# Sliding-window attention feeding a gated MLP: batch 2 transposed by TensorE, batch 3's x^T by DMA, and PSUM homes moved at the end of tile 0

## The chip, the cores and the metric

The kernel runs on one core of a Trainium2 chip. The metric is the device time of one execution in microseconds; of several executions the median is given. The engines of the core work side by side, each on its own queue in program order: TensorE (PE, matrix products and transposes, results to PSUM), VectorE (DVE), ScalarE (ACT), GpSimd (POOL, here casts and DMA issues) and SyncE (SP, here DMA issues).

## What is computed

Attention over a causal window of 64 positions, for 8 batches, 8 heads, 576 positions and head size 64; its output, as 4608 rows of 512, goes through two weight matrices with a gate between them.

```
scores = scale * np.matmul(q, k.transpose(0, 1, 3, 2))
rel = pos[:, None] - pos[None, :]
mask = (rel >= 0) & (rel < window)
...
attn_out = np.matmul(attn, v)
x = np.ascontiguousarray(attn_out.transpose(0, 2, 1, 3)).reshape(B * S, H * D)
h = x @ w_in
g = h * np.clip(h + 3.0, 0.0, 6.0) / 6.0
out = g @ w_out
```

Here w_in is 512 x 2048 and w_out is 2048 x 512. All inputs and the output are float32; the kernel multiplies in bf16.

## The kernel before

The MLP works on 9 tiles of 512 rows (T = 0 to 8), the attention on 8 batches of 576 rows, each as 4 pairs of heads (g = 0 to 3). The order of all work is written by hand: the kernel turns automatic scheduling off, so each engine does its instructions in the order of the code, and only the waits between engines are put in automatically.

**A tile.** Stage 1 (`s1`) makes 16 blocks of 128 hidden units: four matmuls over xT and w_in into a PSUM bank, then the gate: ACT writes relu(h/6 + 1/2), and DVE takes its minimum with 1, times h, into gT. Stage 2 (`s2`) makes 4 output blocks of 128 rows, each in 4 quarters of four matmuls over gT and w_out; ACT copies a finished block to SBUF (`osb`), and SP writes it out (those of tile 0 are held back for POOL's queue).

**A batch.** q, k and v are loaded (SP, for the first two batches partly POOL), cast to bf16 by POOL into `qn_all`, `kn_all` and V, and q and k are transposed into QT and KT, either by PE (`TT` for a pair: four transposes each of q and k, copied from PSUM by DVE and ACT; `RR` for the 64 rows of each that the 512 of the main part leave) or by a DMA transpose on SP. `SS` makes a pair's scores in st0 and st1, takes exp on ACT and masks on DVE. `N_` multiplies with V, both heads of a pair, and DVE normalizes into `opg`. x^T, the input of stage 1, is made from opg by `X_` (five transposes on PE, a copy by ACT) or by `xt_dma` (a DMA transpose on SP).

**What is laid between what.** `stage_(T, ...)` runs stage 1 and stage 2 of a tile, and after block or quarter i it runs the attention pieces that `pieces` lists for i. Tile T carries the attention of batch T + 1. Tile 0 is written out by hand: its stage 2 carries batch 1 and the rest of batch 0. In tiles 1 and 2 of the kernel before, the first four blocks of stage 1 are computed over part of xT first, with pair 3's `X_` in between (`s1` with `first`).

**Data of batches 1 to 4.** Batch 1 comes in rows of 1 KB (`LoadsForPE`, four positions of a head in a row) and is transposed by PE. Batch 2 comes in blocks of 128 positions with rows of 256 bytes (`load_for_dma`: 5 DMAs each for q, k and v), is cast by `cast_for_dma`, and `transpose_pairs_by_dma` issues 8 DMA transposes for it on SP. The loads for batch 3 stand behind them on SP's queue. Batch 3 and those after it are transposed by two DMAs each (`transpose_by_dma`). x^T of batches 0 to 3 is made by PE, that of batches 4 to 7 by DMA.

**PSUM.** Eight banks: st0 and st1 are tiles of two banks each ([P, 2, 512] in float32 or [P, 2, 1024] in bf16), o and acc one bank each, and two h banks that are taken in turn (`h_bank`, `h_tr`). `oa` and `oa_tr` hand out o and acc in turn; `st_tr(u)` and `st_pair(u)` hand out the two halves of st0 or st1. `s1_bank` says where a block of stage 1 is computed; in tile 1 blocks 4 to 15 are in h, h, st0, st1, h, h, st0, st1, o, acc, h, h.

Of the kernel before, what the change touches and what calls it, by code (L numbers as in the profile page):

```python
# [10 lines left out]
BF16 = mybir.dt.bfloat16  # L11
# [13 lines left out]
def kernel(  # L25
# [9 lines left out]
    nc = tc.nc  # L35
    P = nc.NUM_PARTITIONS
# [3 lines left out]
    NG = H // 2  # L40
# [57 lines left out]
        return out  # L98

    class LoadsForPE:  # L100
        def __init__(self, b):
            self.b = b
            self.qst = stage.tile([P, H, R * D], F32, name="qst", tag="qst")
            self.kst = stage.tile([P, H, R * D], F32, name="kst", tag="kst")
            self.rst = stage.tile([P, H, D], F32, name="rst", tag="rst")
            self.tiles = (self.qst, self.kst, self.rst)

        def main(self, i, h0, h1):
            nc.gpsimd.dma_start(
                out=self.tiles[i][:, h0:h1, :],  # L110
                in_=(q, k)[i][self.b, h0:h1, 0:SM, :].rearrange("h (p j) d -> p h (j d)", j=R),
            )

        def rest(self):
            for i, src in enumerate((q, k)):
                nc.gpsimd.dma_start(
                    out=self.rst[i * SR : (i + 1) * SR, :, :],
                    in_=src[self.b, :, SM:S, :].rearrange("h s d -> s h d"),
                )

    def load_v_by_head(b):
        vst = stage.tile([P, KB, H, D], F32, name="vst", tag="vst")
        ins = load_blocks(vst, v, b, (KB - 1,), SR) + load_v(b, vst, 0, H)
        return vst, ins

    def load_for_dma(b):
        sts, ins = [], []
        for n, src in (("qst", q), ("kst", k), ("vst", v)):
            t = stage.tile([P, KB, H, D], F32, name=n, tag=n)
            ins += load_blocks(t, src, b, range(KB), SR if src is v else 0)  # L130
            sts.append(t)
        return tuple(sts), ins
# [108 lines left out]
    class Batch:  # L241
# [28 lines left out]
        def transpose_by_dma(self):  # L270
            for n, T in ((qn_all, self.QT), (kn_all, self.KT)):
# [1 line left out]
                    out=T[:].rearrange("d g (k s) -> d (g k) s", s=P),  # L273
                    in_=n[:].rearrange("p g k h d -> p (g k h d)"),
                )

        def transpose_pairs_by_dma(self):
            for g in range(NG):
                for n, T in ((qn_all, self.QT), (kn_all, self.KT)):
                    nc.sync.dma_start_transpose(  # L280
                        out=T[:, g, :].rearrange("d (k s) -> d k s", s=P),
                        in_=n[:, g, :, :, :].rearrange("p k h d -> p (k h d)"),
                    )

        def cast_qk(self, st, i, h0, heads, copy):
            n = (qn_all, kn_all)[i][:].rearrange("p g k h d -> p (g k h d)")[:, 0 : R * H * D]
# [126 lines left out]
    def xt_pe(bt, g, tr):  # L413
        opg = opgs.pop((bt.b, g))
        n = S if bt.b else SM
        for qb in range(KB if bt.b else KB - 1):
            nc.tensor.transpose(  # L417
                out=tr[:, qb * P : (qb + 1) * P],
                in_=opg[:, qb, :, :].rearrange("p h d -> p (h d)"),
                identity=ident[:],  # L420
            )
        return lambda: acopy(out=xT[:, g, bt.b * S : bt.b * S + n], in_=tr[:, 0:n])
# [38 lines left out]
    def rest_x(bt, u):  # L461
        tr = ps_st.tile([P, 2, 1024], BF16, name=f"st{u}")[:, 0, :]
        for g in range(NG):
            nc.tensor.transpose(
                out=tr[:, g * SR : (g + 1) * SR],
                in_=opr[0:SR, g, :, :].rearrange("p h d -> p (h d)"), identity=ident[0:SR, 0:SR],
            )
        acopy(
            out=xT[:, :, bt.b * S + SM : (bt.b + 1) * S],
            in_=tr[:, 0 : NG * SR].rearrange("d (g s) -> d g s", s=SR),  # L470
        )
# [19 lines left out]
    def h_tr():  # L491
        return ps_h.tile([P, 1024], BF16, name=h_name())
# [31 lines left out]
    def s1(T, first=()):  # L524
        t0 = T * TB
        gT = gpool.tile([P, NFC, TB], BF16, name="gT")
        gTs[T] = gT

        def mms(fc, hT, gs):
            for g in gs:  # L530
                nc.tensor.matmul(  # L531
                    hT, lhsT=win16[:, g, fc * P : (fc + 1) * P],
                    rhs=xT[:, g, t0 : t0 + TB], start=(g == 0), stop=(g == NG - 1),
                )

        def gate(out, hT, shape):
            t1 = (t1pool, t2pool)[len(shape) - 2].tile(shape, BF16, name=f"t{len(shape) - 1}")
            nc.scalar.activation(out=t1[:], in_=hT, func=RELU, bias=half[:], scale=1.0 / 6.0)  # L538
            nc.vector.scalar_tensor_tensor(  # L539
                out=out, in0=t1[:], scalar=1.0, in1=hT, op0=MIN, op1=MULT,  # L540
            )

        if first:
            sts = [ps_st.tile([P, 2, 512], F32, name=f"st{u}") for u in range(2)]
            for gs in first:
                for fc in range(4):
                    mms(fc, sts[fc // 2][:, fc % 2, :], gs)
                yield
            for u in range(2):
                for fc in (2 * u, 2 * u + 1):  # L550
                    mms(fc, sts[u][:, fc % 2, :], (NG - 1,))
                gate(gT[:, 2 * u : 2 * u + 2, :], sts[u][:], [P, 2, TB])
                yield
                yield
        for fc in range(4 if first else 0, NFC):
            hT = s1_bank(fc, T)
            mms(fc, hT, range(NG))
            gate(gT[:, fc, :], hT, [P, TB])
            yield
# [53 lines left out]
    def N_(bt, g, banks=None):  # L613
        n = [pv(bt, g, h, next(banks) if banks else h_bank()) for h in range(2)]
        n[0]()
        n[1]()

    def X_(bt, g, st=None):
        xt_pe(bt, g, h_tr() if st is None else ps_st.tile([P, 2, 1024], BF16, name=f"st{st}")[:, 0, :])()

    def TT(bt, g, banks=None):
        T_(bt, g, banks)
# [118 lines left out]
    bt.cast_v_end(vst1, pcopy)  # L741
    for g in range(NG):
        bt.cast_v(vst1, 2 * g, 2 * g + 2, pcopy)
    st2, _ = load_for_dma(2)

    def st_tr(u):
        t = ps_st.tile([P, 2, 1024], BF16, name=f"st{u}")
# [2 lines left out]
    def st_pair(u):  # L750
        t = ps_st.tile([P, 2, 512], F32, name=f"st{u}")
        return iter((t[:, 0, :], t[:, 1, :]))
# [7 lines left out]
    def go(n=1):  # L760
        run(m, n)
# [6 lines left out]
    S1_(0, 1, 1)  # L768
    go()
    S1_(1, 1, 0)  # L770
    go()
    TT(bt, 2, st_tr(1))
    go()
    TT(bt, 3, st_tr(0))
    go()
    S1_(2, 0, 1)
# [13 lines left out]
    N_(bt, 0, st_pair(0))  # L790
    go()
    N_(bt, 1, oa)
    rest_x(bt0, 1)
    go()
    X_(bt, 0)
    N_(bt, 2, st_pair(0))
    X_(bt, 1, 1)
    N_(bt, 3, oa)
    X_(bt, 2)

    def stage_(T, bt, pieces1, pieces2):
        if T < 3:
            m = s1(T, ((0, 1), (2,)))
            run(m, 1)
            X_(Batch(T), NG - 1)
            run(m, 1)
        else:
            m = s1(T)
        for i in range(NFC):
            run(m, 1)  # L810
            for f in pieces1.get(i, ()):
                f()
        m = s2(T, BY_BLOCK)
        for i in range(16):
            run(m, 1)
            for f in pieces2.get(i, ()):
                f()

    def pieces(bt):
        if bt is None:  # L820
            return {}, {}
        f = lambda fn, *a: lambda: fn(bt, *a)
        p1, p2 = {}, {}
        if bt.b == 2:
            return p1, {
                1: [f(SS, 0)], 2: [f(SS, 1)], 4: [f(N_, 0), f(SS, 2)], 6: [f(X_, 0)], 7: [f(N_, 1), f(SS, 3)],
                9: [f(X_, 1)], 10: [f(N_, 2)], 12: [f(X_, 2)], 13: [f(N_, 3)],
            }
        if bt.b == 3:
            return {13: [f(SS, 0)]}, {  # L830
                0: [f(SS, 1)], 3: [f(N_, 0), f(SS, 2)], 5: [f(X_, 0)], 6: [f(N_, 1), f(SS, 3)],
                8: [f(X_, 1)], 9: [f(N_, 2)], 11: [f(X_, 2)], 12: [f(N_, 3)], 14: [f(X_, 3)],
            }
        p1 = {10: [f(SS, 0)], 13: [f(SS, 1)]}
        p2 = {
            0: [f(SS, 2)], 1: [f(N_, 0)], 2: [f(SS, 3)], 3: [f(N_, 1), f(xt_dma, 0)],
            5: [f(xt_dma, 1)], 6: [f(N_, 2)], 8: [f(N_, 3), f(xt_dma, 2)], 10: [f(xt_dma, 3)],
        }
        return p1, p2

    bt2 = Batch(2)
    bt2.cast_for_dma(st2, (0, 1))
    for u0, osb in held:
        nc.gpsimd.dma_start(out=out[u0 : u0 + P, :], in_=osb[:])
    bt2.cast_for_dma(st2, (2,))
    bt2.transpose_pairs_by_dma()
    nxt, pend = bt2, None
    for T in range(1, NTB):
        p1, p2 = pieces(nxt)
        b = T + 2  # L850
        nxt = None
        if b < B:
            sts, _ = load_for_dma(b)
            nxt = Batch(b)
            p1.setdefault(12 if T == 1 else 6, []).append(
                lambda bt=nxt, sts=sts: bt.cast_for_dma(sts)
            )
            p2.setdefault(6 if T < 3 else 12, []).append(lambda bt=nxt: bt.transpose_by_dma())
        stage_(T, None, p1, p2)


# [28 lines left out]
```

The softmax here doesn't subtract the row's maximum and nothing guards it: scores larger than these inputs give would overflow.

## Time and profile before

| what | value |
|---|---|
| median of 7 runs | 314.17 us (312.67 to 315.31) |
| the profiled execution | 314.43 us, span 312.7 us |
| DMA moved | 52.80 MB, mean 169 GB/s |
| matmuls of stage 2 into o and acc (L568) | 64.1 us and 62.4 us busy |
| matmuls of stage 1 into h (L531) | 62.8 us busy |
| POOL's idle time before its casts of q (L258) | 71.4 us, of it 55.2 us until loads of q landed |
| DMA issues of q, k and v on SP, 256 KB each | 4.7 us, 5.6 us and 5.5 us to landing (median) |
| DMA transposes QT and KT on SP | 9 each, 4.4 us to landing (median) |
| DMA transposes of x^T on SP | 16, 2.9 us to landing (median) |

The span is the time from the first to the last instruction of the profiled execution; the run's own time lies 1.7 us above it. Busy time counts the time in which an engine has an instruction under way. A name such as L322 is a line of the kernel; "gT<-t,st" reads as output from inputs. In a timeline a row has its start, its duration and, in brackets, the idle time of its engine just before it with the instruction that ended that wait. In a table by windows, the columns are the stretch, its length, then busy time and number of instructions of PE, PE's weight loads, DVE, ACT and POOL, then the granted share of PE's clock, the DMA share and GB/s.

### The profile page before, as it was taken

The page shows a single profiled execution, that of the slowest core. Times are in us where ns is not written, and L with a number is a line of the kernel's source. Part 1 is how long each engine was busy: PE and PEld are TensorE (multiplying, and loading weights), DVE is VectorE, ACT ScalarE, POOL GpSimd, SP SyncE. Part 2 cuts the span into 40 slices and gives each one's busy share as a digit, 9 for nine tenths or more (in the row PEclk, how much of TensorE's full clock was granted, in tenths as well). Part 3 has the DMA queues.
Part 4 walks back from the last instruction along what each step waited for, and adds up shares of the span by engine and source line. Part 5 has one row for each costly group of instructions (what it writes and reads, how often), then busy time and mean ns, then how long its engine had stood idle before and what let it go on. Part 6 is the DMA issues. An engine that isn't in the chain of part 4 may idle for free.

```text
span 312.7 us, 5579 instructions
## 1 busy us (share of the span) xinstructions
PE 299.3 (96%) x2125; PEld 148.1 (47%) x2162; DVE 174.8 (56%) x334; ACT 177.4 (57%) x264; POOL 92.2 (29%) x137
## 2 busy tenths in 40 slices
PE   8899898999999999999999999999999999999995
PEld 3454345544654455445544554455445544444442
DVE  4569445485636754478447753775377527306700
ACT  3858654587627854796158715881588157317611
POOL 5876616373044243305600660075000000000000
PEclk9999999999999999999999999999999999999999
DMA  7999999998899999999999999999900630010011
GB/s 243 209 219 238 244 204 201 198 202 220 168 199 199 277 215 195 221 244 203 210 231 212 204 202 230 213 213 190 249 8 2 133 88 0 34 69 34 0 69 67
DMA packets 147579, 52.80 MB, mean 169 GB/s; under 512 B 136384, under 2 KB 142528, under 8 KB 147552
## 3 DMA queue, kind: packets, MB, share of 16 engines
q1 hardware_dynamic: 141920, 44.18, 70.4%
q0 software_dynamic: 5360, 8.00, 12.6%
q8 instruction: 17, 0.28, 0.4%
q10 hardware_dynamic: 272, 0.26, 0.2%
q14 instruction: 10, 0.08, 0.1%
HBM read 36.70 MB, written 9.44 MB: 148 GB/s over the span
## 4 chain that ended last, share of the span: by engine, by line
PE 73%; DMA 14%; SPq 4%; POOL 3%; DVE 2%; ACT 1%; issue 1%; POOLq 0%
PE o L568 17%; PE acc L568 16%; PE h L531 15%; PE o L531 5%; PE acc L531 5%; PE st L531 5%; DMA wout<-in_moe_w_out_dram 4%; PE st L354 3%; DMA kst<-in_k_dram 3%; DMA qst<-in_q_dram 3%; DMA vst<-in_v_dram 3%; SPq L94 2%; PE h L384 2%; DMA KT<-kn 1%; PE h L389 1%
## 5 line engine op out<-in xcount | busy, mean ns | idle before, releaser
L531 PEld LDWEIGHTS <-win 128*128 128x128 bf16 x576 | 55.2, 98 | 66.8 <-issue 1.6
L568 PEld LDWEIGHTS <-gT 128*128 128x128 bf16 x576 | 52.4, 98 | 57.2 <-issue 1.0
L568 PE MATMUL o<-wout,gT 128*128 128x512 bf16 x261 | 64.1, 380 | 1.4 <-DMA wout<-in_moe_w_out_dram 0.6
L531 PE MATMUL h<-xT,win 128*128 128x512 bf16 x259 | 62.8, 379 | 0.3
L568 PE MATMUL acc<-wout,gT 128*128 128x512 bf16 x261 | 62.4, 379 | 0.6
L362 ACT ACTIVATE pT<-st 128x768 bf16<-128x768 f32 x64 | 48.7, 808 | 14.2 <-PE st L354 14.1
L539 DVE SCALAR_TENSOR_TENSOR gT<-t,st 128x512 bf16<-128x512 bf16 (+1 forms) x26 | 20.7, 809 | 57.1 <-ACT t L538 57.0
L538 ACT ACTIVATE t<-h,half 128x512 bf16<-128x512 f32 x66 | 44.7, 690 | 8.4 <-PE h L531 7.9
L539 DVE SCALAR_TENSOR_TENSOR gT<-t,h 128x512 bf16<-128x512 bf16 x66 | 44.5, 685 | 7.9 <-ACT t L538 7.7
L372 DVE TENSOR_TENSOR pT<-pT,mask 128x1536 bf16<-128x1536 bf16 x28 | 28.3, 1011 | 22.6 <-ACT pT L362 22.6
L258 POOL CAST qn<-qst 128x512 bf16<-128x512 f32 x24 | 16.6, 730 | 71.4 <-DMA qst<-in_q_dram 55.2
L574 ACT COPY osb<-acc 128x512 f32<-128x512 f32 x17 | 10.0, 586 | 41.2 <-PE acc L568 41.2
L531 PE MATMUL st<-xT,win 128*128 128x512 bf16 x124 | 29.9, 379 | 0.9 <-DVE gT L539 0.3
L574 ACT COPY osb<-o 128x512 f32<-128x512 f32 x17 | 10.0, 588 | 30.4 <-PE o L568 30.4
L406 DVE TENSOR_TENSOR opg<-h,rec 128x320 bf16<-128x320 f32 x48 | 23.6, 491 | 1.7
L531 PE MATMUL o<-xT,win 128*128 128x512 bf16 x91 | 23.6, 379 | 0.4 <-DVE gT L539 0.3
L538 ACT ACTIVATE t<-st,half 128x512 bf16<-128x512 f32 (+1 forms) x26 | 20.1, 785 | 6.7 <-PE st L531 6.4
L531 PE MATMUL acc<-xT,win 128*128 128x512 bf16 x90 | 23.5, 379 | 0.1
L248 POOL CAST V<-vst 128x512 bf16<-128x512 f32 (+1 forms) x14 | 16.6, 1189 | 16.9 <-DMA vst<-in_v_dram 14.3
L384 PEld LDWEIGHTS <-pT 128*128 128x128 bf16 x256 | 17.4, 97 | 7.6 <-PE h L417 0.5
L258 POOL CAST kn<-kst 128x512 bf16<-128x512 f32 x24 | 14.6, 648 | 17.7 <-DMA kst<-in_k_dram 14.0
L354 PE MATMUL st<-QT,KT 64*128 64x192 bf16 (+2 forms) x312 | 17.5, 230 | 1.6 <-DMA KT<-kn 0.7
(107 smaller groups left out, 282.3 us busy)
## 6 DMA issues: line engine op xcount, KB each, us to landing
out_dram<-osb SPq DMA_DIRECT2D x32, 256.0 KB, 2.5
qst<-in_q_dram SPq DMA_DIRECT2D x28, 256.0 KB, 4.7
kst<-in_k_dram SPq DMA_DIRECT2D x27, 256.0 KB, 5.6
vst<-in_v_dram SPq DMA_DIRECT2D x24, 256.0 KB, 5.5
vst<-in_v_dram SPq DMA_DIRECT2D x23, 128.0 KB, 3.6
win<-in_moe_w_in_dram POOLq DMA_DIRECT2D x4, 512.0 KB, 8.0
wout<-in_moe_w_out_dram POOLq DMA_DIRECT2D x4, 512.0 KB, 13.0
qst<-in_q_dram POOLq DMA_DIRECT2D x2, 512.0 KB, 11.9
```

Source lines behind the costliest of these rows:

```text
L248: copy(out=self.V[:, 0 : KB - 1, h0:h1, 0:D], in_=vst[:, 0 : KB - 1, h0:h1, :])
L258: pcopy(out=n[:, g, 0 : KB - 1, :, :].rearrange("p k h d -> p k (h d)"), in_=s[:, 0 : KB - 1, 2 * g : 2 * g + 2, :].rearrange("p k h d -> ...
L354: nc.tensor.matmul(st[:, h, o0 : o0 + n], lhsT=bt.KT[h * D : (h + 1) * D, g, k0 : k0 + P], rhs=bt.QT[h * D : (h + 1) * D, g, q0 : q0 + n], ...
L362: nc.scalar.activation(out=pT[:, :, 2 * u : 2 * u + 2, 0:QW], in_=st[:, :, 0:w].rearrange("p h (k w) -> p h k w", k=2), func=EXP, scale=scale,
L372: nc.vector.tensor_tensor(out=pT[:, :, :, 0:QW], in0=pT[:, :, :, 0:QW], in1=mask[:].rearrange("p (h k) w -> p h k w", h=2), op=MULT,)
L384: nc.tensor.matmul(ob, lhsT=pT[:, h, qb, 0:P], rhs=V[:, qb, 2 * g + h, :], start=True, stop=(qb == 0),)
L406: nc.vector.tensor_tensor(out=opgs[bt.b, g][:, 0:nb, h, :], in0=ov[:, :, 0:D], in1=rec[:, 0:nb].unsqueeze(2).to_broadcast([P, nb, D]), op= ...
L531: nc.tensor.matmul(hT, lhsT=win16[:, g, fc * P : (fc + 1) * P], rhs=xT[:, g, t0 : t0 + TB], start=(g == 0), stop=(g == NG - 1),)
L538: nc.scalar.activation(out=t1[:], in_=hT, func=RELU, bias=half[:], scale=1.0 / 6.0)
L539: nc.vector.scalar_tensor_tensor(out=out, in0=t1[:], scalar=1.0, in1=hT, op0=MIN, op1=MULT,)
L568: nc.tensor.matmul(accs[ts], lhsT=gT[:, fc, ts * P : (ts + 1) * P], rhs=wout16[:, fc, :], start=(fc == 0), stop=(fc == NFC - 1),)
L574: acopy(out=osb[:], in_=accs[ts])
```

## The change

- Batch 2 is loaded as batch 1 is, in rows of 1 KB, but on SP's queue (`LoadsForPE` gets an engine), q and k for the first four heads first; V comes head by head. It is cast by `cast_pairs` and `cast_rest`.
- Its 8 DMA transposes go (`transpose_pairs_by_dma` is removed). PE transposes it in tile 1: pairs 0 and 1 in stage 1 after blocks 6 and 10, in o and acc; pairs 2 and 3 and the remaining rows in stage 2 after quarters 0, 3 and 1, in the h banks. Its scores and products move one or two quarters later.
- Batch 3 loses its own list of pieces and gets that of the later batches: scores after blocks 10 and 13 of tile 2's stage 1, x^T by four DMAs on SP. Its casts are placed in tile 1's stage 2 after quarter 6, its DMA transposes after quarter 8; those of batch 4 move to stage 2's quarter 12.
- At the end of tile 0: `TT` of batch 1's pair 2 stands one quarter earlier; `rest_x` of batch 0 uses st0; `X_` of pairs 0 and 1 share the tile st1; `N_` of pair 2 uses o and acc, of pair 3 the h banks; `X_` of pairs 2 and 3 move into tile 1, where the first four blocks of stage 1 are computed over xT group 0, then 1, then 2. Tile 2 is cut in the same way, with `X_` of batch 2's pairs 2 and 3.

```diff
--- before.py
+++ after.py
@@ -98,22 +98,22 @@
         return out
 
     class LoadsForPE:
-        def __init__(self, b):
-            self.b = b
+        def __init__(self, b, eng=None):
+            self.b, self.eng = b, eng or nc.gpsimd
             self.qst = stage.tile([P, H, R * D], F32, name="qst", tag="qst")
             self.kst = stage.tile([P, H, R * D], F32, name="kst", tag="kst")
             self.rst = stage.tile([P, H, D], F32, name="rst", tag="rst")
             self.tiles = (self.qst, self.kst, self.rst)
 
         def main(self, i, h0, h1):
-            nc.gpsimd.dma_start(
+            self.eng.dma_start(
                 out=self.tiles[i][:, h0:h1, :],
                 in_=(q, k)[i][self.b, h0:h1, 0:SM, :].rearrange("h (p j) d -> p h (j d)", j=R),
             )
 
         def rest(self):
             for i, src in enumerate((q, k)):
-                nc.gpsimd.dma_start(
+                self.eng.dma_start(
                     out=self.rst[i * SR : (i + 1) * SR, :, :],
                     in_=src[self.b, :, SM:S, :].rearrange("h s d -> s h d"),
                 )
@@ -274,14 +274,6 @@
                     in_=n[:].rearrange("p g k h d -> p (g k h d)"),
                 )
 
-        def transpose_pairs_by_dma(self):
-            for g in range(NG):
-                for n, T in ((qn_all, self.QT), (kn_all, self.KT)):
-                    nc.sync.dma_start_transpose(
-                        out=T[:, g, :].rearrange("d (k s) -> d k s", s=P),
-                        in_=n[:, g, :, :, :].rearrange("p k h d -> p (k h d)"),
-                    )
-
         def cast_qk(self, st, i, h0, heads, copy):
             n = (qn_all, kn_all)[i][:].rearrange("p g k h d -> p (g k h d)")[:, 0 : R * H * D]
             copy(
@@ -615,8 +607,8 @@
         n[0]()
         n[1]()
 
-    def X_(bt, g, st=None):
-        xt_pe(bt, g, h_tr() if st is None else ps_st.tile([P, 2, 1024], BF16, name=f"st{st}")[:, 0, :])()
+    def X_(bt, g, banks=None):
+        xt_pe(bt, g, next(banks) if banks else h_tr())()
 
     def TT(bt, g, banks=None):
         T_(bt, g, banks)
@@ -741,7 +733,14 @@
     bt.cast_v_end(vst1, pcopy)
     for g in range(NG):
         bt.cast_v(vst1, 2 * g, 2 * g + 2, pcopy)
-    st2, _ = load_for_dma(2)
+    ld = LoadsForPE(2, nc.sync)
+    ld.main(0, 0, 4)
+    ld.main(1, 0, 4)
+    ld.rest()
+    ld.main(0, 4, 8)
+    ld.main(1, 4, 8)
+    st2 = ld.tiles
+    vst2, _ = load_v_by_head(2)
 
     def st_tr(u):
         t = ps_st.tile([P, 2, 1024], BF16, name=f"st{u}")
@@ -768,9 +767,8 @@
     S1_(0, 1, 1)
     go()
     S1_(1, 1, 0)
-    go()
     TT(bt, 2, st_tr(1))
-    go()
+    go(2)
     TT(bt, 3, st_tr(0))
     go()
     S1_(2, 0, 1)
@@ -790,19 +788,28 @@
     N_(bt, 0, st_pair(0))
     go()
     N_(bt, 1, oa)
-    rest_x(bt0, 1)
-    go()
-    X_(bt, 0)
-    N_(bt, 2, st_pair(0))
-    X_(bt, 1, 1)
-    N_(bt, 3, oa)
-    X_(bt, 2)
+    rest_x(bt0, 0)
+    go()
+    two = st_tr(1)
+    X_(bt, 0, two)
+    X_(bt, 1, two)
+    N_(bt, 2, oa)
+    N_(bt, 3)
 
     def stage_(T, bt, pieces1, pieces2):
-        if T < 3:
-            m = s1(T, ((0, 1), (2,)))
+        if T == 1:
+            m = s1(T, ((0,), (1,), (2,)))
             run(m, 1)
-            X_(Batch(T), NG - 1)
+            X_(Batch(1), 2, oa_tr)
+            run(m, 1)
+            X_(Batch(1), 3, oa_tr)
+            run(m, 1)
+        elif T == 2:
+            m = s1(T, ((0,), (1,), (2,)))
+            run(m, 1)
+            X_(Batch(2), 2)
+            run(m, 1)
+            X_(Batch(2), 3)
             run(m, 1)
         else:
             m = s1(T)
@@ -822,14 +829,10 @@
         f = lambda fn, *a: lambda: fn(bt, *a)
         p1, p2 = {}, {}
         if bt.b == 2:
-            return p1, {
-                1: [f(SS, 0)], 2: [f(SS, 1)], 4: [f(N_, 0), f(SS, 2)], 6: [f(X_, 0)], 7: [f(N_, 1), f(SS, 3)],
-                9: [f(X_, 1)], 10: [f(N_, 2)], 12: [f(X_, 2)], 13: [f(N_, 3)],
-            }
-        if bt.b == 3:
-            return {13: [f(SS, 0)]}, {
-                0: [f(SS, 1)], 3: [f(N_, 0), f(SS, 2)], 5: [f(X_, 0)], 6: [f(N_, 1), f(SS, 3)],
-                8: [f(X_, 1)], 9: [f(N_, 2)], 11: [f(X_, 2)], 12: [f(N_, 3)], 14: [f(X_, 3)],
+            return {6: [f(TT, 0, oa_tr)], 10: [f(TT, 1, oa_tr)]}, {
+                0: [f(TT, 2)], 1: [f(RR)], 2: [f(SS, 0)], 3: [f(TT, 3)], 4: [f(SS, 1)],
+                6: [f(N_, 0), f(SS, 2)], 8: [f(X_, 0)], 9: [f(N_, 1), f(SS, 3)],
+                11: [f(X_, 1)], 12: [f(N_, 2)], 14: [f(N_, 3)],
             }
         p1 = {10: [f(SS, 0)], 13: [f(SS, 1)]}
         p2 = {
@@ -839,11 +842,14 @@
         return p1, p2
 
     bt2 = Batch(2)
-    bt2.cast_for_dma(st2, (0, 1))
+    cast_pairs(bt2, st2, 0, 4)
+    bt2.cast_rest(st2, pcopy)
+    cast_pairs(bt2, st2, 4, 4)
     for u0, osb in held:
         nc.gpsimd.dma_start(out=out[u0 : u0 + P, :], in_=osb[:])
-    bt2.cast_for_dma(st2, (2,))
-    bt2.transpose_pairs_by_dma()
+    bt2.cast_v_end(vst2, pcopy)
+    for g in range(NG):
+        bt2.cast_v(vst2, 2 * g, 2 * g + 2, pcopy)
     nxt, pend = bt2, None
     for T in range(1, NTB):
         p1, p2 = pieces(nxt)
@@ -852,10 +858,10 @@
         if b < B:
             sts, _ = load_for_dma(b)
             nxt = Batch(b)
-            p1.setdefault(12 if T == 1 else 6, []).append(
+            (p2 if T == 1 else p1).setdefault(6, []).append(
                 lambda bt=nxt, sts=sts: bt.cast_for_dma(sts)
             )
-            p2.setdefault(6 if T < 3 else 12, []).append(lambda bt=nxt: bt.transpose_by_dma())
+            p2.setdefault(8 if T == 1 else 12, []).append(lambda bt=nxt: bt.transpose_by_dma())
         stage_(T, None, p1, p2)
 
 
```

## The prediction

> **What bounds the kernel now.** I read the engine rows first, then busy time by stage, then PE's timeline, then what ACT and DVE do where PE's order changes.
>
> ```profile
> span 312.7 us, 5579 instructions
> PE 299.3 (96%) x2125; PEld 148.1 (47%) x2162; DVE 174.8 (56%) x334; ACT 177.4 (57%) x264; POOL 92.2 (29%) x137
> ...
> 38.90:58.70 19.80, 17.47 (x190) 9.84 (x191) 11.64 (x29) 9.96 (x16) 7.08 (x14) 1.00 1.14 201
> 94.80:108.00 13.20, 12.14 (x64) 5.42 (x64) 9.16 (x13) 10.61 (x16) 4.52 (x6) 1.00 1.02 235
> 158.40:190.10 31.70, 31.49 (x229) 15.58 (x232) 19.67 (x36) 18.50 (x28) 10.24 (x13) 1.00 1.11 212
> ```
>
> PE (first busy column) is the bound at the full granted clock. A later tile is busy 31.49 of 31.70 us. Where the change acts, PE idles 2.33 us in 38.9 to 58.7 and 1.06 us in 94.8 to 108.0. By the first matmuls of each stage 1, tile 1 lasts from 58.07 to 92.06 (33.99 us), tile 2 to about 126.62 (34.56), tile 3 to 158.38 (31.76). So there is little to win: a saving counts only if it takes work or a recorded wait from PE, and a new PE wait counts in full.
>
> ```profile
> 39.53 1.02 PE L568 MATMUL o<-wout,gT 128*128 128x512 bf16 x4 [0.59 <-DMA wout<-in_moe_w_out_dram]
> 40.39 0.39 PE L317 MATMUL st<-ident,qn 128*128 128x128 bf16 x4
> 40.61 0.39 PE L317 MATMUL st<-ident,kn 128*128 128x128 bf16 x4
> 40.83 1.03 PE L568 MATMUL acc<-wout,gT 128*128 128x512 bf16 x4
> ...
> 57.78 0.45 PE L417 MATMUL h<-ident,opg 128*128 128x128 bf16 x5 [0.67 <-DVE opg L406]
> ...
> 105.78 0.51 PE L354 MATMUL st<-QT,KT 64*128 64x192 bf16 x10 [0.70 <-DMA KT<-kn]
> ```
>
> Columns are start, duration, instruction, and in brackets the idle time with its releaser. Eight transposes run from 40.39 to 40.83, so one costs 55 ns of PE; a quarter block of stage 2 (four matmuls) costs 0.86 us. The three brackets are the waits that the change can reach.
>
> **PE work.** Batch 2 on PE needs 4 pairs x 2 x 4 transposes and 4 for the remaining rows: 36 x 0.055 = +1.98 us, all in tile 1. Batch 3's x^T by DMA takes 4 x 5 away: 20 x 0.055 = -1.10 us, in tile 2. The other x^T groups only change places. Net +0.88 us. A rule speaks against this trade: the Trainium skill ("TensorE: Matmul & The Clock Gate", Part 4: PE-mode transpose) gives about 275 ns for a 128x128 bf16 transpose inside a kernel. Sixteen more would be 4.4 us by that figure and 0.88 by the row. The row decides: it is start to start, in this kernel, between the same matmuls.
>
> **Waits that go.** (1) Moving the transposes of batch 1's pair 2 ahead of the quarter block that waits for w_out fills that gap: the previous scores end near 38.9, the bank st1 is free (its exp ran 37.73 to 38.54), the weights land at 39.48 either way, so the 0.44 us of transposes come free: -0.44. (2) X of pair 2 in batch 1 waited 0.67 for DVE; now four matmuls of tile 1 stand in front of it: -0.67. X of pair 3, behind four more, should still wait about 0.1 for its own normalization: +0.12. (3) Batch 3's scores waited 0.70 for KT at 105.78. Its loads were issued from 79.22 on, because SP had eight transposes of batch 2 in front. Those are gone; SP can issue batch 3's loads as soon as the tiles are cast, near 60 to 76. Its POOL casts now stand behind PE's last read of qn (about 80), two casts of 2.9 us follow, then two SP transposes of some 3 us each with landing: about 93, where scores now start near 106. -0.70. (4) Two score groups one quarter apart cost 0.20 at 76.68 (waiting on the exp); they now stand two apart: -0.20. Together -1.89, with X of pair 3 included.
>
> **New waits**, all for a PSUM bank. These rows of ACT and DVE carry them:
>
> ```profile
> 41.03 0.69 DVE L322 COPY QT<-st 128x512 bf16<-128x512 bf16 x1 [0.26 <-PE st L317]
> ...
> 41.76 0.58 ACT L322 COPY KT<-st 128x512 bf16<-128x512 bf16 x1 [1.97 <-DVE QT L322]
> ...
> 55.62 0.58 ACT L574 COPY osb<-h 128x512 f32<-128x512 f32 x1 [0.60 <-PE h L568]
> 56.10 0.65 ACT L422 COPY xT<-h 128x576 bf16<-128x576 bf16 x1
> ...
> 69.52 0.69 DVE L539 SCALAR_TENSOR_TENSOR gT<-t,st 128x512 bf16<-128x512 bf16 x1 [0.18 <-ACT t L538]
> ...
> 73.84 0.69 DVE L539 SCALAR_TENSOR_TENSOR gT<-t,h 128x512 bf16<-128x512 bf16 x1 [0.18 <-ACT t L538]
> ```
>
> (a) X of pairs 0 and 1 of batch 1 get the two halves of st1. The first two rows show such a tile: q's transposes in one half, k's in the other. DVE's copy of q waited for k's transposes (end 40.83), and ACT's copy of k waited for DVE's copy of q (41.72): the tile is handed over as a whole. Then pair 1's transposes wait until ACT has copied pair 0: transposes end 55.69, ACT is still at the output block, its copy runs 56.10 to 56.75, PE goes on at 56.80: +1.1 us. Queued behind it are N of pairs 2 and 3 and the whole of tile 1. The skill's rule ("PSUM — Partial Sum Buffer", PSUM bank collisions raise a hardware error) is to guard by bank; halves of 2 KB are two banks, so by the rule this wait would be 0 and the total +0.7 us, by the row +1.8. I take the row: it is the same kind of tile, twice in the trace. Ends 0 and 1.1.
>
> (b) In tile 1's stage 1, pair 1 of batch 2 is transposed into o and acc after block 10, and block 12 is computed in o. DVE copies q only after block 10's gate (it starts at 69.52; queued operations follow 0.60 apart): copy 70.12 to 70.81, PE at 70.87. PE would come to block 12 at 69.46 + 0.44 = 69.90: +0.97 us. Pair 0 after block 6 has no block in o or acc behind it; DVE takes its 0.60 in the 0.26 us a block has spare. Ends 0 and 1.2.
>
> (c) Pair 2 goes to the h banks after the first quarter of stage 2, while block 15's gate still reads one: 73.84 + 0.69, so PE may go on at 74.6 and stands ready at 72.92 + 0.86 + 0.22 = 74.0: +0.61. Ends 0.4 and 0.8.
>
> (d) The remaining rows are copied by DVE (0.28) and then ACT (0.37) out of one bank; with 0.2 before and 0.1 behind, that is 0.96 us against the 0.86 us quarter that covers it: +0.10. The moved rest_x, now in st0, waits for a normalization that ended at 54.43 where it stood at 54.32: under 0.1, nothing.
>
> **Behind other work.** Batch 2's loads: SP begins them at 49.69. POOL's 512 KB loads with 1 KB rows landed 1.45 us apart (35.72, 37.16), SP's 256 KB blocks 1.2 us apart. So pairs 0 and 1 of q and k land near 56, are cast (1.04 us each) by 58, the rest by 62; PE asks at about 64.2 and, for pair 2, at 74. Cover 6 us. V is cast by 70, behind the four output issues of POOL, and asked for after 81. The x^T DMAs of batch 3 stand on SP behind batch 4's loads, which start near 95 and not at 105.77, so SP is free near 113 when the first is due; in tile 3 the same four issued as late as 151.10 to 155.73 and the last landed at 158.33, just in time for 158.38. The casts of batch 4 also move earlier. No gain follows in tiles 3 to 8: their PE has 0.2 us of idle time each.
>
> **Sum.** +0.88 of work, -1.89 of waits, new waits 1.1 + 0.97 + 0.61 + 0.10 = +2.78: **+1.8 us** on the profiled execution's 314.43 (span 312.7 and 1.7 around it) is 316.2; on the median of 314.17 it is **316.0 us**.
>
> **Rivals.** *Halves tracked apart*: only (a) goes, +0.7, 314.9 us; for it, the halves are different banks; against it, the KT row. *Data late*: if the SP loads behaved like POOL's in the weight phase (11.9 us to landing, against 3.4 to 6.3 on SP), q and k of pairs 0 and 1 would be cast near 64 and those after them near 70, each a few us later than I put it; from about 7 us later on PE stops in stage 1, and 2 us of that give 318. Against it: the weights have landed by 46.7. *Faster*: the PSUM homes are free in time, because DVE takes q's copies ahead of gates that still wait for ACT and PE comes later to the shared banks: then work +0.88 and -2.01 remain, 313.0 us. It decides once the new waits are below 0.2 us together; for it, DVE is only 56% busy; against it, DVE's order is fixed by hand, gate first.
>
> **Chances.** The sum above 0.58, halves apart 0.20, faster 0.12, data late 0.10. What can be told from no change here is 0.3%, 0.94 us either side of 314.17. The first case lies mostly above 315.1 (0.53 of 0.58), halves apart mostly within the band (0.13 of 0.20, the rest above), data late above: slower 0.69, same 0.19, faster 0.12. The likeliest case alone spans 315.0 to 317.2; the range to hold eight in ten reaches down into the second case and up towards the late data: 313.9 to 317.6.
>
> **What would show it.** After: pair 1's X transposes idle about 1.1 us, released by ACT's xT copy; block 12 into o idle 1 us, released by QT; k's transposes of pair 2 idle 0.6, released by gT; no wait of L354 for KT by DMA; tile 1 near 37.6 us long, tile 2 near 32.7, tile 3 unchanged at 31.8. I am wrong if PE waits on POOL or on loads in tile 1, if the bank waits are absent, or if tile 2 keeps its length.

## The result, and the profile after

The changed kernel takes 316.08 us (median of 26 executions, 314.74 to 318.17); the kernel before, run beside it, 314.17 us (63 executions). The ratio is 1.0063, with a 95% interval of 1.0047 to 1.0079: about 2.0 us slower, between 1.5 and 2.5.

In the changed kernel the line numbers have moved: L523 is a matmul of stage 1, L560 of stage 2, L309 a transpose of q or k, L409 one of x^T, L364 the masked product. Its page begins:

```profile
span 316.4 us, 5620 instructions
PE 301.9 (95%) x2140; PEld 149.5 (47%) x2178; DVE 178.2 (56%) x339; ACT 176.6 (56%) x265; POOL 97.9 (31%) x138
```

Its busy time by stage (columns as before, PE is the first busy one; the rows are stage 2 of tile 0, tile 1 and tile 2):

```profile
37.03:59.92 22.89, 21.02 (x213) 11.23 (x216) 11.19 (x26) 12.55 (x20) 9.13 (x15) 1.00 1.08 213
59.92:96.93 37.01, 35.09 (x288) 18.83 (x291) 25.07 (x46) 22.59 (x34) 20.92 (x30) 1.00 1.11 215
96.93:129.82 32.89, 32.28 (x240) 16.20 (x242) 19.36 (x35) 18.82 (x28) 10.22 (x13) 1.00 1.00 181
```

PE is busy 2.6 us longer than before, over a span that is 3.7 us longer. Tile 2 is 1.7 us shorter, tile 1 is 3.0 us longer. These are waits in PE's timeline that the profile before does not have. The change made the last three; the first, for the weights w_in, is not its work:

```profile
20.02 3.10 PE L523 MATMUL st<-xT,win 128*128 128x512 bf16 x7 [1.83 <-DMA win<-in_moe_w_in_dram]
...
58.67 0.44 PE L409 MATMUL st<-ident,opg 128*128 128x128 bf16 x5 [0.94 <-ACT xT L414]
...
73.30 1.02 PE L523 MATMUL o<-xT,win 128*128 128x512 bf16 x4 [0.79 <-DVE QT L314]
...
78.41 0.38 PE L309 MATMUL h<-ident,kn 128*128 128x128 bf16 x4 [0.41 <-DVE gT L531]
```

At 58.67 the second x^T of the shared tile waits for ACT's copy of the first; at 73.30 block 12 waits in o for DVE's copy of q; at 78.41 pair 2's k waits for the gate of block 15. The wait for KT by DMA is gone. In this one execution w_in came late, and PE then ran at half its clock for a while; that is no part of the change (the section on the hardware comes back to it). Two more profiles of the same kernel show PE busy for 300.9 and 300.4 us, 1.6 and 1.1 us more than before. Lengths in us, from the first matmul of each stage to the next:

| stretch | before | after | after, 2nd | after, 3rd |
|---|---|---|---|---|
| start to stage 2 of tile 0 | 33.63 | 37.03 | 33.44 | 33.90 |
| stage 2 of tile 0 | 24.44 | 22.89 | 23.56 | 23.00 |
| tile 1 | 33.99 | 37.01 | 37.02 | 37.02 |
| tile 2 | 34.62 | 32.89 | 33.92 | 33.81 |
| tile 3 to the end | 186.02 | 186.55 | 186.97 | 186.66 |

Tile 1 is the same to 0.01 us in all three. Tile 2 is not, and why is the second question of the experiments.

### The profile page after: what moved, and what is told of

It reads as the page before. It is cut to its first block, busy times and chain, and to the rows that moved or that the text cites. A ratio compares the mean times of both kernels' runs of the same rounds, so it can differ in the third digit from the quotient of the medians.

```text
span 316.4 us, 5620 instructions
## 1 busy us (share of the span) xinstructions
PE 301.9 (95%) x2140; PEld 149.5 (47%) x2178; DVE 178.2 (56%) x339; ACT 176.6 (56%) x265; POOL 97.9 (31%) x138
## 4 chain that ended last, share of the span: by engine, by line
PE 85%; DMA 7%; DVE 2%; ACT 2%; SPq 2%; issue 1%; POOL 0%; POOLq 0%
PE acc L560 18%; PE o L560 18%; PE h L523 17%; PE st L523 8%; PE acc L523 6%; PE o L523 6%; PE st L346 4%; DMA qst<-in_q_dram 3%; DMA win<-in_moe_w_in_dram 2%; PE h L376 2%; PE h L381 1%; PE h L560 1%; SPq L94 1%; DMA vst<-in_v_dram 1%; DVE gT L531 1%
## 5 line engine op out<-in xcount | busy, mean ns | idle before, releaser
L523 PEld LDWEIGHTS <-win 128*128 128x128 bf16 x576 | 55.4, 98 | 68.3 <-issue 3.7
L560 PEld LDWEIGHTS <-gT 128*128 128x128 bf16 x576 | 52.5, 98 | 57.0 <-issue 0.5
L560 PE MATMUL o<-wout,gT 128*128 128x512 bf16 x261 | 64.3, 380 | 0.6 <-issue 0.2
L523 PE MATMUL h<-xT,win 128*128 128x512 bf16 x259 | 63.0, 379 | 0.3
L560 PE MATMUL acc<-wout,gT 128*128 128x512 bf16 x261 | 61.9, 379 | 0.7 <-issue 0.2
L531 DVE SCALAR_TENSOR_TENSOR gT<-t,st 128x512 bf16<-128x512 bf16 (+1 forms) x26 | 20.7, 808 | 61.9 <-ACT t L530 61.8
L364 DVE TENSOR_TENSOR pT<-pT,mask 128x1536 bf16<-128x1536 bf16 x28 | 30.3, 1083 | 20.9 <-ACT pT L354 20.8
L258 POOL CAST qn<-qst 128x512 bf16<-128x512 f32 x20 | 13.0, 689 | 71.8 <-DMA qst<-in_q_dram 46.5
L523 PE MATMUL st<-xT,win 128*128 128x512 bf16 x124 | 32.1, 393 | 2.3 <-DMA win<-in_moe_w_in_dram 1.8
L398 DVE TENSOR_TENSOR opg<-h,rec 128x320 bf16<-128x320 f32 x50 | 24.6, 491 | 1.7
L523 PE MATMUL o<-xT,win 128*128 128x512 bf16 x91 | 23.6, 379 | 1.1 <-DVE QT L314 0.8
L523 PE MATMUL acc<-xT,win 128*128 128x512 bf16 x89 | 23.5, 379 | 0.2
L248 POOL CAST V<-vst 128x512 bf16<-128x512 f32 (+1 forms) x17 | 18.1, 1067 | 14.1 <-DMA vst<-in_v_dram 10.7
L258 POOL CAST kn<-kst 128x512 bf16<-128x512 f32 x20 | 15.3, 802 | 10.7 <-DMA kst<-in_k_dram 10.7
L346 PEld LDWEIGHTS <-KT 64*128 64x128 bf16 x312 | 10.9, 94 | 15.7 <-issue 12.7
```

The costliest lines, as they stand in the source:

```text
L248: copy(out=self.V[:, 0 : KB - 1, h0:h1, 0:D], in_=vst[:, 0 : KB - 1, h0:h1, :])
L258: pcopy(out=n[:, g, 0 : KB - 1, :, :].rearrange("p k h d -> p k (h d)"), in_=s[:, 0 : KB - 1, 2 * g : 2 * g + 2, :].rearrange("p k h d -> ...
L346: nc.tensor.matmul(st[:, h, o0 : o0 + n], lhsT=bt.KT[h * D : (h + 1) * D, g, k0 : k0 + P], rhs=bt.QT[h * D : (h + 1) * D, g, q0 : q0 + n], ...
L364: nc.vector.tensor_tensor(out=pT[:, :, :, 0:QW], in0=pT[:, :, :, 0:QW], in1=mask[:].rearrange("p (h k) w -> p h k w", h=2), op=MULT,)
L398: nc.vector.tensor_tensor(out=opgs[bt.b, g][:, 0:nb, h, :], in0=ov[:, :, 0:D], in1=rec[:, 0:nb].unsqueeze(2).to_broadcast([P, nb, D]), op= ...
L523: nc.tensor.matmul(hT, lhsT=win16[:, g, fc * P : (fc + 1) * P], rhs=xT[:, g, t0 : t0 + TB], start=(g == 0), stop=(g == NG - 1),)
```

## The experiments

Eleven runs were made, in three groups (the first four, the next four, the last three), each group on one chip with the kernel before beside it. All ratios are to the kernel before. The three profiles of the kernel after stand above: the second is the first run here, the third is the ninth.

**The changed kernel again.**

> The changed kernel again, as the measure for the three others on the same chip. My theory (three new PSUM waits, then work, make up the loss): about 316.1 us, ratio 1.006 to the kernel before, with the waits of 0.9, 0.8 and 0.4 us that the changed profile shows. Rival (the loss lies in the start: the changed profile shows a wait of 1.83 us for w_in at 20.02, which the kernel before did not have): the late w_in is there again and the start up to the first quarter of tile 0's stage 2 is some 2 us longer than before.

316.4 us, ratio 1.0064 (1.0046 to 1.0082). The start was 33.44 us long, no longer than before, and the waits of 0.94, 0.79 and 0.41 us were all there. The loss isn't in the start.

**Own tiles for the two x^T.**

```diff
-    two = st_tr(1)
-    X_(bt, 0, two)
-    X_(bt, 1, two)
+    X_(bt, 0, st_tr(0))
+    X_(bt, 1, st_tr(1))
```

> X of pairs 0 and 1 of batch 1 get a tile of their own each (first half of st0, first half of st1). My theory: the wait of 0.94 us of the second X for ACT's copy of the first goes, nothing takes its place, about 315.1 us (ratio 1.003). Rival (halves are free of each other, and the wait was ACT being late with the output block): the wait stays in another form and the time stays at 316.1. Rival (the start): 316.1.

315.61 us, ratio 1.0038 (1.0019 to 1.0057). The wait of 0.94 us is gone and none stands in its place (one of 0.69 us earlier in the stage, for batch 0's KT, is 0.24 in the changed kernel's profiles and varies); tile 1 is unchanged at 37.01. In time it is 0.8 us less, though the intervals of the two kernels overlap. Same two engines, same order, only separate tiles: ACT's lateness alone was not the cause.

**Other banks for blocks 12 to 15.**

```diff
-        if fc in (12, 13):
-            return (ps_o, ps_acc)[fc - 12].tile([P, 512], F32, name=("o", "acc")[fc - 12])[:]
         if fc % 4 < 2:
             return h_bank()[:]
-        return ps_st.tile([P, 2, 512], F32, name=f"st{fc % 2}")[:, 0, :] if fc < 12 else h_bank()[:]
+        return ps_st.tile([P, 2, 512], F32, name=f"st{fc % 2}")[:, 0, :]
```

> Blocks 12 to 15 of tile 1's stage 1 go to h, h, st0, st1 and no longer to o, acc, h, h. My theory: the wait of 0.79 us of block 12 for DVE's copy of q goes, and so does the one of 0.41 us of pair 2's k transposes for block 15's gate: 1.2 us less, about 314.9 us (ratio 1.002). Rival (DVE is simply behind in that stretch): PE stops at another bank instead, at block 13 or 14 or at the first scores of batch 2, and at most 0.4 us is won. Rival (the start): 316.1.

314.86 us, ratio 1.0019 (0.9997 to 1.0041), 1.4 us less than the changed kernel; the two intervals do not overlap. PE's timeline of this kernel at the two places (L521 is stage 1, L558 stage 2):

```profile
68.64 1.03 PE L521 MATMUL st<-xT,win 128*128 128x512 bf16 x4
69.50 1.89 PE L521 MATMUL h<-xT,win 128*128 128x512 bf16 x8
71.23 1.89 PE L521 MATMUL st<-xT,win 128*128 128x512 bf16 x8
72.95 1.03 PE L558 MATMUL o<-wout,gT 128*128 128x512 bf16 x4
73.82 0.39 PE L309 MATMUL h<-ident,qn 128*128 128x128 bf16 x4
74.04 0.39 PE L309 MATMUL h<-ident,kn 128*128 128x128 bf16 x4
```

Block 12 follows block 11 without idle time, and k's transposes follow q's by 0.22 us. Tile 1 went from 37.02 to 35.58. DVE isn't behind in that stretch: PE had come to two banks too early.

**Both edits.**

> Both edits together. My theory: the savings add up, 2.1 us less than the changed kernel, about 314.0 us: no difference from the kernel before, with net 0.9 us of transposes more and 1.3 to 1.8 us of old waits gone. Rival (the start): 316.1.

313.4 us, ratio 0.997 (0.9946 to 0.9994): 0.3% faster than the kernel before. The interval excludes no change, though narrowly. Against the changed kernel it is 2.95 us less by the ratios, more than the 2.1 us of waits and than the 0.8 and 1.4 us of the single edits. In the traces, stage 2 of tile 0 and tile 1 together are 2.2 to 2.8 us shorter than in the changed kernel's three; what goes beyond the three waits is not explained.

**Pair 2 of batch 1 transposed one quarter later again.**

```diff
     S1_(1, 1, 0)
+    go()
     TT(bt, 2, st_tr(1))
-    go(2)
+    go()
```

> The changed kernel with one step undone: batch 1's pair 2 is transposed one quarter later in tile 0, as before. My theory (these 0.44 us of transposes fill a wait for w_out that PE has in any case): 0.3 to 0.45 us slower than the changed kernel, about 316.8 us, and PE waits 0.3 to 0.6 us for w_out again. Rival (the weights land by then in most executions, so the gap is not there to be filled): as the changed kernel, 316.4 us.

316.51 us, ratio 1.0082 (1.0049 to 1.0115). By the ratios 0.6 us slower than the changed kernel, from six executions, which is not told apart from nothing. In the trace the wait is back:

```profile
38.97 1.02 PE L560 MATMUL o<-wout,gT 128*128 128x512 bf16 x4 [0.68 <-DMA wout<-in_moe_w_out_dram]
```

Of the eleven traces of kernels that keep the step, nine have 0.13 us or less there, but batch 3's old list (below) has 0.45 and the changed kernel with V in four has 0.81:

```profile
40.30 1.02 PE L561 MATMUL o<-wout,gT 128*128 128x512 bf16 x4 [0.81 <-DMA wout<-in_moe_w_out_dram]
```

So the step fills the gap in most executions and not in all; it depends on when w_out lands and when PE comes to it. That it saves 0.44 us is not shown.

**Batch 3's x^T on PE at the places of the DMAs.**

```diff
         p1, p2 = {}, {}
...
+        if bt.b == 3:
+            return {10: [f(SS, 0)], 13: [f(SS, 1)]}, {
+                0: [f(SS, 2)], 1: [f(N_, 0)], 2: [f(SS, 3)], 3: [f(X_, 0), f(N_, 1)],
+                5: [f(X_, 1)], 6: [f(N_, 2)], 8: [f(X_, 2), f(N_, 3)], 10: [f(X_, 3)],
+            }
```

> The changed kernel, but x^T of batch 3 is made by PE again (20 transposes and 4 copies by ACT), at about the places where the DMAs were issued; the data of batch 3 still come early. My theory (PE is the bound): 1.1 us slower than the changed kernel, 317.5 us, and no wait for KT by DMA. Rival (the four DMAs on SP crowd the loads of batch 4 and its casts, and cost in tiles 2 and 3 what they save): as the changed kernel or faster, 316.0 to 316.5 us.

318.69 us, ratio 1.0149 (1.0123 to 1.0176): 2.7 us slower than the changed kernel, more than either theory said. Its PE timeline tells why:

```profile
116.88 0.22 PE L376 MATMUL h<-V,pT 128*128 128x65 bf16 x2 [0.91 <-ACT xT L414]
...
119.25 0.45 PE L409 MATMUL h<-ident,opg 128*128 128x128 bf16 x5 [0.25 <-DVE opg L398]
...
123.79 0.22 PE L376 MATMUL h<-V,pT 128*128 128x65 bf16 x2 [0.48 <-ACT xT L414]
```

My new order put N directly behind x^T, and both use the h banks: the first and the last of these waits, 1.39 us. The middle one, 0.25 us, is for a normalization that DVE began only after a masked product of 2.10 us (the run on V, below, has to do with that). With the 1.1 us of transposes they make the 2.7. So the run doesn't price the change's step; the run with the old list, further down, comes nearer to that.

**q and k of batch 2 in rows of 256 bytes.**

```diff
+            if self.b == 2:
+                for j in range(R):
+                    self.eng.dma_start(
+                        out=self.tiles[i][:, h0:h1, j * D : (j + 1) * D],
+                        in_=(q, k)[i][self.b, h0:h1, 0:SM, :].rearrange("h (p j) d -> p h j d", j=R)[:, :, j, :],
+                    )
+                return
```

> The changed kernel with q and k of batch 2 loaded in rows of 256 bytes into the same places (four DMAs in place of one). My theory (these loads have 4 us or more of cover and bound nothing): the time of the changed kernel, 316.4 us. Rival (rows of 1 KB are what lets PE have batch 2 in time): the loads land 1 to 3 us later, PE waits for POOL's casts in tile 1, 317 us or more.

315.28 us, ratio 1.0047 (1.0026 to 1.0068): not slower. No wait for POOL appeared in tile 1, which took 37.02 us. The rival came true in its first half: the last of k landed 15.1 us after the first issue of q, where it took 10.6 to 13.4 in the eleven traces with rows of 1 KB. The time before PE asks for them covers that, so the rows don't matter for the time here.

**V cast in four pieces, with both edits.** In two of the first group's traces tile 2 took 33.9 us, in one 33.1 and in one 32.8, with the same work. The difference is a masked product of DVE. POOL and DVE of the changed kernel, second profile, and what PE waited for then:

```profile
115.41 1.90 POOL L248 CAST V<-vst 128x2048 bf16<-128x2048 f32 x1 [3.26 <-PE h L387]
117.37 1.22 POOL L250 CAST V<-vst 64x512 bf16<-64x512 f32 x1
...
115.61 2.50 DVE L364 TENSOR_TENSOR pT<-pT,mask 128x1536 bf16<-128x1536 bf16 x1 [0.55 <-ACT pT L354]
...
118.80 0.23 PE L376 MATMUL h<-V,pT 128*128 128x65 bf16 x2 [0.56 <-DVE opg L398]
```

The product starts 0.2 us after POOL's cast of V and ends 0.8 us after the cast's end at 117.31; alone it takes 0.96 us. The cast behind it takes 1.22 in place of 0.61. In the changed kernel's first profile the order is the other way round: the product starts at 118.62 and takes its 0.96, and the cast takes 2.59 in place of 1.90.

```profile
118.74 2.59 POOL L248 CAST V<-vst 128x2048 bf16<-128x2048 f32 x1 [2.91 <-PE h L387]
```

The Trainium skill has this rule ("SBUF — State Buffer", Who interferes with whom): a DVE instruction with two SBUF inputs contends with a GpSimd instruction that reads SBUF, and whoever comes first blocks the other. The numbers agree with a block, not with a slower rate for both: the one that came first kept its usual time, and the other ended 0.80 us (product) or 1.75 us (cast) after it, some 0.15 us less than its usual time.

```diff
             if 2 in which:
-                self.cast_v(st[2], 0, H, pcopy)
+                for g in range(NG):
+                    self.cast_v(st[2], 2 * g, 2 * g + 2, pcopy)
                 self.cast_v_end(st[2], pcopy)
```

> The kernel with both edits (own homes for X, other banks for blocks 12 to 15), and POOL casts V of batches 3 to 7 in four pieces of two heads (0.62 and 0.29 us each) in place of one of 1.90 us. Theory (DVE's masked product and a cast of POOL exclude each other, so that a product that starts just behind the long cast takes 2.5 us in place of 0.96, which PE pays for in tile 2): no masked product over about 1.5 us, tile 2 always 32.8 us, 0.2 to 0.5 us faster than with both edits alone, about 313.1 us. Rival (the long products are covered by PE's other work, and tile 2 varies for another reason): 313.4 us, tile 2 between 32.8 and 33.9.

312.83 us, ratio 0.9971 (0.9954 to 0.9988); no product of tile 2 over 1.34 us, tile 2 at 32.91. In time it can't be told from both edits alone (0.997), so the gain that I expected is not shown; the gain over the kernel before is there again, on another chip.

**The changed kernel for the third time.**

> The changed kernel once more, as the measure for the two others on this chip: 316.2 us, ratio 1.006. Tile 2 is 32.8 us long where no masked product of it takes over 1.2 us, and up to 33.9 where one takes 2.5.

316.5 us, ratio 1.0066 (1.0043 to 1.009), from six executions; the product took 2.39 us, tile 2 33.81.

**Batch 3's old list.** The list of the kernel before, as the diff of the change shows it, put in front of the common one.

```diff
+        if bt.b == 3:
+            return {13: [f(SS, 0)]}, {
+                0: [f(SS, 1)], 3: [f(N_, 0), f(SS, 2)], 5: [f(X_, 0)], 6: [f(N_, 1), f(SS, 3)],
+                8: [f(X_, 1)], 9: [f(N_, 2)], 11: [f(X_, 2)], 12: [f(N_, 3)], 14: [f(X_, 3)],
+            }
```

> The changed kernel with batch 3's list of pieces exactly as before the change: x^T by PE at its old places, scores after blocks 13 and later; its data still come early. My theory (PE is the bound, and the 2.7 us that x^T on PE cost in the earlier run were 1.1 us of transposes and 1.6 us of waits at places that were not made for it): 1.1 us slower than the changed kernel, 317.3 us, no wait for KT by DMA, tile 2 near 33.9. Rival (x^T on PE costs more than its transposes wherever it stands, through the copies by ACT and the h banks): 2 us or more slower, 318.2 us.

317.24 us, ratio 1.0092 (1.0063 to 1.0122): 0.8 us by the ratios, near the 1.1 of the transposes; the intervals overlap with the changed kernel's, so the size is not shown by time alone. Tile 2 took 34.12, 1.2 to 1.3 us more than with x^T by DMA and an undisturbed product, and PE waited for nothing over 0.3 us there. The rival's 2 us do not appear: where it has room, x^T on PE costs about its transposes.

**The changed kernel with V in four, and nothing else.** The same diff as two above.

> The changed kernel with nothing but POOL's cast of V (batches 3 to 7) cut into four. Theory (the cast that excludes DVE's masked product is what makes tile 2 longer in some executions): no masked product over 1.5 us, tile 2 at 32.8 us, 0.3 to 0.6 us faster than the changed kernel. Rival (covered): the same time, as with both edits, where it made no difference that the measurement could tell.

315.97 us, ratio 1.0048 (1.0031 to 1.0065), by the ratios 0.6 us faster than the changed kernel in the same group; the intervals overlap, so the time alone does not show a gain. The trace is as expected: tile 2 took 32.79, and the product that met the cast before now starts behind a short one.

```profile
116.38 0.62 POOL L248 CAST V<-vst 128x512 bf16<-128x512 f32 x1 [3.39 <-DMA vst<-in_v_dram]
117.07 0.96 POOL L250 CAST V<-vst 64x128 bf16<-64x128 f32 x1
...
116.91 0.96 DVE L365 TENSOR_TENSOR pT<-pT,mask 128x1536 bf16<-128x1536 bf16 x1 [0.55 <-ACT pT L355]
```

All traces with batch 3's x^T by DMA, ordered by how long that product (of pair 3 of batch 3) took:

| kernel | product, us | tile 2, us |
|---|---|---|
| changed with V in four | 0.96 | 32.79 |
| rows of 256 bytes | 0.96 | 32.80 |
| other banks | 0.96 | 32.82 |
| changed, 1st | 0.96 | 32.89 |
| both edits, V in four | 1.03 | 32.91 |
| both edits | 1.70 | 33.13 |
| pair 2 later | 1.99 | 33.59 |
| changed, 3rd | 2.39 | 33.81 |
| own tiles | 2.50 | 33.91 |
| changed, 2nd | 2.50 | 33.92 |

The longer the product, the longer the tile, up to 1.1 us. Which of the two engines comes first is a matter of 0.2 us of phase (in the changed kernel's first profile DVE began 0.12 us before the cast), so one kernel has both in different executions. A long product costs only where PE soon needs what stands behind it on DVE: in tile 1 the product of batch 2's pair 3 meets batch 3's cast of V and took 2.13, 1.09 and 1.82 us in the three profiles of the changed kernel, with tile 1 at 37.01 or 37.02 in all.

## Why the prediction was right

The total, +1.8 us, was measured at +2.0 (1.5 to 2.5). The mechanism was right: PE at its bound pays for its new work and for three new bank waits, and the edits that take these waits away take the loss away. That the total came within 0.2 us is in part luck. By stages, in us of difference to the profile before:

| stretch | the prediction's terms | after | after, 2nd | after, 3rd |
|---|---|---|---|---|
| stage 2 of tile 0 | -0.3 | -1.55 | -0.88 | -1.44 |
| tile 1 | +3.6 | +3.02 | +3.03 | +3.03 |
| tile 2 | -1.5 | -1.73 | -0.70 | -0.81 |
| tile 3 to the end | 0 | +0.53 | +0.95 | +0.64 |
| together | +1.8 | +0.27 | +2.40 | +1.42 |

The terms are too high in tile 0 and tile 1 and, but for tile 2 of the first profile, too low behind; the two nearly cancel.

- **PE's work.** Tile 1 without bank waits (other banks, 35.58 us) is 1.6 us longer than before: 1.98 of transposes, less the 0.20 for the scores one quarter apart, less some 0.2 of which I found no cause (x^T of batch 1's pair 2 comes in and that of batch 2's pair 2 goes out, 0.28 each). No run undoes these transposes alone; their price stands on this length. At the 275 ns that the Trainium skill gives ("TensorE: Matmul & The Clock Gate", Part 4: PE-mode transpose), 36 transposes would have been 9.9 us, an estimate from its figure.
- **(a) shared st1**: 1.1 predicted, 0.94 in every trace with the shared tile, gone with own tiles. The rule by bank, from which I read a wait of 0, says what has to be guarded at least; this kernel's waits are drawn by tile. The rival *halves tracked apart* falls.
- **(b) block 12 in o**: 0.97 predicted, 0.79 measured. **(c) k of pair 2**: 0.61 predicted, 0.41 measured. **(d)** 0.10 and the 0.12 of X of pair 3: no wait in any trace. Each hand-over was set 0.16 to 0.20 us too long, and two small waits did not come; tile 1 came out at 37.0, not 37.6.
- **Waits that went**: that of batch 1's x^T for DVE and that for KT are in no trace. The w_out gap is filled in the three profiles of the changed kernel, but not in every trace that has the step. Stage 2 of tile 0 became 0.9 to 1.6 us shorter where my terms make 0.3 (-0.44, -0.67, 0.28 moved out, +1.1): in the second profile the rest lies in two waits that are not the same in every execution, 0.62 before and 0.21 in the second profile for the remaining rows of batch 1, 0.44 and 0.24 for batch 0's KT.
- **Tile 2**: 32.7 predicted, which leaves out the 0.28 us of x^T of batch 2's pair 2 that comes in (33.1 with it); 32.8 to 32.9 where the masked product is undisturbed, up to 33.9 where it meets POOL's cast of V. The step that failed is the sentence on POOL, "The casts of batch 4 also move earlier. No gain follows in tiles 3 to 8": I looked for a gain there and not for a collision. In the profile before, batch 4's cast of V ran at 126.50, where no masked product stands to be blocked; now it runs at 115 to 119, among the products of tile 2.
- **Data late** falls: q and k of pairs 0 and 1 had landed by 54.2 and 56.0 in the second profile, the rest by 61.8, and PE never waited for POOL in tile 1. **Faster** falls for this kernel; with the new waits taken away by the choice of homes it comes true in the kernel with both edits, at 313.4 where the rival said 313.0.

From tile 3 on the three profiles are 0.5 to 1.0 us longer than before, for which I had put nothing. Tile 3 is part of it: I read it as 31.76 us before, but its first matmul stands at 126.68 and that of tile 4 at 158.22, so it took 31.54, and it takes 31.75 to 32.06 in the three profiles. Another 0.25 lies in the last tile (31.55 in the profile before and in three traces of variants, 31.80 in the changed kernel's). The cause of both is open. With batch 3's x^T on PE the stretch took 186.31 and 186.08 us, near the 186.02 before; in the ten traces with it by DMA it took 186.44 to 187.07, but no run was made to settle that.

So the change as it stands pays more for its PSUM homes than it gains elsewhere. By the prediction's terms its work and its removed waits come to -1.1 us; placing the PSUM homes cost 2.1 us by the traces, and the two edits of homes alone turn a loss of 0.6% into a gain of 0.3%.

## What to carry to other kernels

When work for PE is put between blocks that are written by hand, follow the PSUM home of each new result to its next user, and count the queue of the engine that empties it: three such hand-overs made the whole loss here, and choosing other homes removed them. Two results in one tile were handed over together here though they lie in different banks; give them tiles of their own. When loads come earlier, so do the casts behind them; look at what runs on DVE at the new time.

## What the runs showed of the hardware that I had not expected

**POOL and DVE block each other** for nearly whole instructions: a masked product of 0.96 us became 2.50 behind a cast of 1.90, and a cast of 1.90 became 2.59 behind a product.

**Row size.** On SP, the first four heads of q took 4.3 us from the first issue to the last landing in rows of 1 KB (one DMA, 49.13 to 53.47, with x^T on PE) and 4.9 in rows of 256 bytes (four DMAs, 48.89 to 53.77). The first four heads of k landed 2.0 and 2.6 us after them. From the first issue to the last landing, all of q and k but the remaining rows took 10.6 to 13.4 us with the long rows (eleven traces) and 15.1 with the short ones (one trace). The short rows also came in four times as many DMAs; which of the two made them later is not told apart. For both I had expected the 1.45 us per 512 KB that POOL's loads showed in the weight phase.

**The clock at the start.** In the first profile PE stood idle from 18.2 to 20.0 for w_in, and then ran at about half its clock for 3.4 us; with own tiles for x^T it stood idle for 1.38 us and kept its clock. By windows, of the changed kernel and then of that one (the column behind POOL is the granted clock):

```profile
18.20:20.00 1.80, 0.00 (x0) 0.11 (x2) 1.59 (x7) 0.58 (x1) 1.80 (x3) 1.00 1.14 175
20.00:23.40 3.40, 3.38 (x12) 1.49 (x12) 0.00 (x0) 0.00 (x0) 3.36 (x6) 0.52 1.21 184
```

```profile
17.70:19.00 1.30, 0.00 (x0) 0.11 (x2) 1.27 (x4) 0.58 (x1) 1.26 (x3) 1.00 1.19 185
19.00:20.70 1.70, 1.62 (x9) 0.80 (x9) 0.56 (x3) 0.00 (x0) 1.70 (x3) 1.00 1.24 203
```

The kernel with both edits shows the same after 1.76 us (granted 0.50). These two profiles have a mean granted clock of 0.995 and 0.993. The kernel before has 0.992 to 0.995 in 16 of its 133 executions beside the experiments, so a loss of that size is no matter of the change. From the start to stage 2 of tile 0 the traces took between 33.1 us (pair 2 later) and 37.0 us (changed, 1st), which is more than the change itself: a single profile of each kernel would have told the wrong story.
